# Attention and two gated layers on one core: one queue of decoding operations in place of parallel decoding, and the next segment's x split one cast at a time

## The chip, the core and the metric

The kernel runs on one core of a Trainium2 chip. The time is that of one execution on the device, in microseconds. The profile is of one execution, taken by the hardware profiler. The engines are TensorE (PE in the profile, its weight loads PEld), VectorE (DVE), ScalarE (ACT), GpSimd (POOL) and SyncE (SP), which issues nearly all DMAs. Each engine works through its own instructions in program order.

## The reference

Three layers in float32: masked attention over 4 batches, 8 heads, 576 positions and 64 dimensions; then two gated layers on 2304 tokens with 512 channels and 1536 hidden units, the first after an RMS norm. Cut to what matters:

```python
attn = softmax(where(mask, q @ k.T / 8, -1e9));  x = attn @ v          # (2304, 512)
xn = x / rms(x) * rms_g
y   = (silu(xn @ w_gate) * (xn @ w_val)) @ w_out                       # moe:  512 -> 1536 -> 512
out = (silu(y @ w2_gate) * (y @ w2_val)) @ w2_out                      # moe2: 512 -> 1536 -> 512
```

## The kernel before, in words

A float32 factor of a product is kept as two parts, a rounded high part and the rest (types F32R), and each product is three matmuls: high by high, high by low, low by high. Hidden units go in chunks of 128, twelve in each layer.

**Early part.** The attention and the first six chunks of the first gated layer run together, over six blocks of tokens (`segs`). The profile shows it up to about 399 us.

**Segments.** The rest is 15 segments (`work`) of 768 tokens: chunks 6 to 8 of the first layer for three blocks of tokens, chunks 9 to 11 for three, and for the second layer chunks 0 to 3, 4 to 7 and 8 to 11, for three blocks each. They are numbered 0 to 14 here; 0 to 5 have 3 chunks and 198 matmuls, 6 to 14 have 4 chunks and 240. In a segment a chunk's gate and value products (2 by 2 blocks of 384 tokens) are formed from seven block products, called steps 1 to 7 (`Chunk.step`), in the order 1, 2, 6, 5, 7, 4, 3. A step is six matmuls. Between steps ACT and DVE copy, add and take the SiLU of banks of PSUM: after step 1 ACT seeds a second bank (`seed`), after 6 and 7 it keeps a copy (`keep`), after 2 and 4 it applies the SiLU, and `join` makes the two parts of the hidden values (`hh` by ACT, `hl` by DVE). Down products follow a chunk or two later (`Half.down`); half of those of a segment are done in the next one (`left`).

**x of the next segment.** `stage_x` loads it into the one buffer `xst`, `sum_x` forms sums on POOL, and `split_q` makes for each of the seven steps two high parts (an ACT cast, `xh`, L984) and two low parts (a POOL subtraction, `xl`, L985). A tile of the split has one buffer, so it can be written once the last chunk of the running segment is past that step.

**Weights.** They are decoded from two 16 bit halves. A load takes one of three `raw` buffers, then come `low` and `high` (ACT, L198 and L190), `sign` and `join` (DVE, L202 and L207), then for each part of 512 or 256 columns a cast on ACT (`hi`, L214) and a subtraction on DVE (`lo`, L218). For the seven-step chunks `combined_step` loads gate and value weights together (two raws), and between decoding and the third cast POOL forms four differences (`sums`, L253). `weight_step` does the down weights. In the second layer `low` can go to a spare bank of PSUM (`lws`). There are 20 places for decoded weights of 4 KB and 5 of 2 KB; a chunk takes four and one, and gives them back when the last segment of its pass has used it.

**What sets the order.** `point()` is called twice in a step and once in each group of down products. There every weight step that is under way advances by one phase (all of them side by side, up to as many as the raw buffers allow), and by `pace["dec"]`, 0.25 per call, the next one is begun. Four empty phases lie between load and first operation. In this kernel the queue for the 18 later chunks holds combined weights and down weights by turns. A scheduler with priorities then orders each engine's instructions; `behind(engine)` keeps an instruction behind the last bank operation recorded for an engine. The next x is split by `split_next(z)` right after the last chunk's step z: four instructions at once, and their ACT casts are not held behind anything.

Of the kernel before, what the change touches and what calls it, by code (L numbers as in the profile page):

```python
# [25 lines left out]
def attn_ffn_ffn(ctx: ExitStack, tc: tile.TileContext, q, k, v, w1g, w1v, w1o, rms_g, w2g, w2v, w2o, out):  # L26
# [91 lines left out]
        if st:  # L118
            active.append(st)

    pace = {"att": 0.0, "dec": 0.0}
    have = {"att": 0.0, "dec": 0.0}

    def point():
        advance()
        for nm, src in (("dec", wq), ("att", steps)):
            if state["hold"] and nm == "dec":
                continue
            have[nm] = min(have[nm] + pace[nm], 2.0)
            while have[nm] >= 1.0 and src and src[0].ready():  # L130
                have[nm] -= 1.0
                start(src.pop(0))
# [87 lines left out]
    def weight_step(m, c, z):  # L220
        cell = {}

        def load():
            cell["at"] = take((m, c, z == 2), 4)
            cell.update(fetch(m, c, z))

        def first():
            cell["t"] = home(cell["at"], 512, f"w{m}_{c}_{z}")
            hi(cell["t"], cell["h"])

        def second():
            lo(cell["t"], cell["h"])
            wt[m, c, z] = cell["t"]
            wdone.add((m, c, z))

        return Step([load] + [wait] * 4 + scale(cell) + [first, second], lambda: room[4] and raws[0] >= 1, PRIO_W)

    def combined_step(m, c):

        g, v = {}, {}  # L240
        at = []

        def load():
            at.extend([take((m, c, False), 4) for _ in range(3)] + [take((m, c, False), 2)])
            g.update(fetch(m, c, 0))
            v.update(fetch(m, c, 1))

        def sums():
            t = g["raw"].rearrange("p k f -> p (k f)").bitcast(F32).rearrange("p (a n) -> p a n", a=4)
            b11, b21 = g["h"][:, 0:256], g["h"][:, 256:512]  # L250
            b12, b22 = v["h"][:, 0:256], v["h"][:, 256:512]
            for z, a, b in ((0, b12, b11), (2, b22, b12), (1, b22, t[:, 0]), (3, b21, t[:, 1])):
                nc.gpsimd.tensor_tensor(out=t[:, z], in0=a, in1=b, op=ALU.subtract)  # L253
            flat = t.rearrange("p a n -> p (a n)")
            g["parts"] = [(g["h"], 512, at[0]), (v["h"][:, 256:512], 256, at[3]), (flat[:, 0:512], 512, at[1]), (flat[:, 512:1024], 512, at[2])]
            g["t"] = []

        def first(i):
            def f():
                src, w, place = g["parts"][i]  # L260
                t = home(place, w, f"w{m}_{c}_{i}")
                g["t"].append(t)
                hi(t, src)
            return f

        def second(i):
            def f():
                lo(g["t"][i], g["parts"][i][0])
                if i == 3:
                    raws[0] += 1  # L270
                    tg, tb, t12, t34 = g["t"]
                    wt[m, c, 0] = {1: tg[:, :, 0:256], 2: tg[:, :, 256:512], 3: tb, 5: t12[:, :, 0:256], 6: t12[:, :, 256:512],
                                   7: t34[:, :, 0:256], 4: t34[:, :, 256:512]}
                    wdone.add((m, c, 0))
            return f

        return Step([load] + [wait] * 4 + scale(g, 0) + scale(v) + [sums, wait] +
                    [f(i) for i in range(4) for f in (first, second)],
                    lambda: len(room[4]) >= 3 and room[2] and raws[0] >= 2, PRIO_W)

# [2 lines left out]
        return tc.issue_after(last[eng]) if eng in last else nullcontext()  # L283

    def need_w(m, c, z):
        drain(wq, lambda: (m, c, z) in wdone)


    class Attention:
# [613 lines left out]
    for si, (m, t0, n, c0, c1) in enumerate(segs):  # L903
        nxt = segs[si + 1] if si + 1 < len(segs) else None
        loaded = False
        pace["att"] = 0.8 if si < 2 else 1.2
        pace["dec"] = 0.5 if si == NA - 1 else 0.25
        xs = xs_of.pop(si)
        state["tanh"] = True and att is not None
        for c in range(c0, c1):  # L910
            h = gate(m, c, n, xs)
            if si == last_seg[m, c]:
                used((m, c, False))
            if len(waiting) >= 2:
                run(waiting.pop(0))
            waiting.append((si, c, h))
            if att and not steps and not active_att():
                actx.close()
                att = None
                GV.append(("a0", "a1"))  # L920
                open_pool("x7", "x7", 0, bufs=1)
                open_pool("wpb", "wpb", 0, bufs=1)
                open_pool("ob", "ob", 512, bufs=4)
                room[4] += [(pools["wpb"][0], f"v{i}") for i in range(2)]
                room[2] += [(pools["wpb"][0], f"e{i}") for i in range(5)]
            if nxt and c >= c1 - 3 and si + 1 not in xs_of:
# [12 lines left out]
    while waiting:  # L939
        run(waiting.pop(0))  # L940
    pace["dec"] = 0.3
    close_pools(0, 1, "h")


# [26 lines left out]

    SRC = {1: "a11", 2: "a12", 3: "a12", 4: "a22", 5: "s1", 6: "a11", 7: "a21"}

    def split_q(cell, i, eng=nc.gpsimd):

        src = cell[SRC[i]]
        if i == 6:
            combine(eng, src, cell["s1"], src, ALU.subtract)
        if i == 3:
            combine(eng, src, src, cell["a11"], ALU.subtract)  # L980
        xh = x7.tile([128, 2, HN], F32R, tag=f"h{i}", name="xh")
        xl = x7.tile([128, 2, HN], F32R, tag=f"l{i}", name="xl")
# [148 lines left out]
    cell = stage_x(1, 0)  # L1131
    sum_x(cell, nc.vector)
    for i in (1, 2, 6, 5, 7, 4, 3):
        split_q(cell, i, nc.vector)
    left = []
    for n, (m, cs, t0) in enumerate(work):
        if t0 == 0:
# [9 lines left out]

        G = [J[:2], J[2:]]

        def split_next(i):  # L1150
            if nxt:
                split_q(cell, i)

        def step(c, z):
            c.step(z)
            if c is chunks[-1]:
                split_next(z)

        def lower(i, g):
            if i >= 0:  # L1160
                for j in G[g]:
                    halves[0].down(chunks[i].c, j, chunks[i].ha)
                point()

        def piece(hf, c, js, done):
            def f():
# [7 lines left out]
        def other_done(m=m, cs=cs, t0=t0):  # L1174
            if t0 + 2 * HN == NT:
                for c in cs:
                    used((m, c, True))

        def blank():
            if left:  # L1180
                left.pop(0)()

        for z in (1, 0, 0, 2, 6, 0, 5, 7, 0):
            step(chunks[0], z) if z else blank()
            if z == 2:
                spare[:] = ya[halves[0].n:]
        for i, c in enumerate(chunks[:-1]):
            c1 = chunks[i + 1]
            step(c1, 1)
            step(c, 4)  # L1190
            step(c, 3)
            if t0 + 2 * HN == NT:
                used((m, c.c, False))
            step(c1, 2)
            if i == 0 and nxt:
# [12 lines left out]
            lower(i, 0)  # L1208
# [12 lines left out]
        lower(k - 1, 0)  # L1221
        lower(k - 1, 1)
        blank()
        while nxt is None and left:
            blank()
    close_pools(*reversed(list(opened)))
# [30 lines left out]
```

## Time and profile before

| | us |
|---|---|
| median of 3 runs | 1063.78 (1061.88 to 1070.92) |
| the profiled execution | 1068.32, span 1065.7 |
| PE busy | 998.5 (94%) |
| PEld, DVE, ACT, POOL busy | 903.5, 584.4, 575.0, 443.0 |
| mean granted TensorE clock | 0.969 of full |

A busy share of PE holds matmuls whose ends are modelled and overlap, so a full window says only that PE was not seen to wait. Of the chain of work that ended last PE has 60% of the span, DMA 11%, ACT 9%, DVE 8%, POOL 7%.

### The profile page before, as it was taken

The page shows a single profiled execution, that of the slowest core. Times are in us where ns is not written, and L with a number is a line of the kernel's source. Part 1 is how long each engine was busy: PE and PEld are TensorE (multiplying, and loading weights), DVE is VectorE, ACT ScalarE, POOL GpSimd, SP SyncE. Part 2 cuts the span into 40 slices and gives each one's busy share as a digit, 9 for nine tenths or more (in the row PEclk, how much of TensorE's full clock was granted, in tenths as well). Part 3 has the DMA queues.
Part 4 walks back from the last instruction along what each step waited for, and adds up shares of the span by engine and source line. Part 5 has one row for each costly group of instructions (what it writes and reads, how often), then busy time and mean ns, then how long its engine had stood idle before and what let it go on. Part 6 is the DMA issues. An engine that isn't in the chain of part 4 may idle for free.

```text
span 1065.7 us, 16395 instructions
## 1 busy us (share of the span) xinstructions
PE 998.5 (94%) x5804; PEld 903.5 (85%) x5804; DVE 584.4 (55%) x1311; ACT 575.0 (54%) x1435; POOL 443.0 (42%) x463
## 2 busy tenths in 40 slices
PE   5758999999999998999899989999989999999998
PEld 4647998788789888898799978999888999889997
DVE  3777546354443767646685587333856337653433
ACT  4877646635623557446565356454846347562431
POOL 3212102103100132785796584643747264654600
PEclk9658999999999998999999999999999999999999
DMA  6575143241132346534644544303273433515021
GB/s 180 167 213 150 56 124 85 84 128 40 41 108 81 112 161 195 173 105 152 208 137 157 178 144 160 109 11 122 86 256 102 155 126 131 196 42 177 23 88 59
DMA packets 130090, 133.85 MB, mean 126 GB/s; under 512 B 41428, under 2 KB 113820, under 8 KB 130008
## 3 DMA queue, kind: packets, MB, share of 16 engines
q1 hardware_dynamic: 129816, 132.53, 38.9%
q8 instruction: 45, 0.74, 0.3%
q14 instruction: 37, 0.30, 0.1%
q0 software_dynamic: 192, 0.28, 0.1%
HBM read 99.75 MB, written 33.03 MB: 125 GB/s over the span
## 4 chain that ended last, share of the span: by engine, by line
PE 60%; DMA 11%; ACT 9%; DVE 8%; POOL 7%; issue 3%; SPq 2%; ACTq 0%; DVEq 0%; POOLq 0%
PE b_y L66 23%; PE b_a L66 14%; PE b_g L66 11%; PE b_v L66 10%; DMA raw<-in_moe_w_out_dram 6%; POOL xl L985 4%; DMA raw<-in_moe_w_gate_dram 2%; PE b_a L69 2%; ACT xh L984 2%; POOL raw L253 2%; DVE dh L207 2%; DMA raw<-in_moe_w_val_dram 2%; ACT w L214 2%; DMA xst<-x_d 1%; ACT raw L198 1%
## 5 line engine op out<-in xcount | busy, mean ns | idle before, releaser
L985 POOL TENSOR_TENSOR xl<-xst,xh 128x384 fp32r<-128x384 f32 x168 | 180.1, 1103 | 75.0 <-ACT xh L984 75.0
L66 PE MATMUL b_y<-xh,w 128*128 128x384 f32 x700 | 191.2, 338 | 10.7 <-ACT t L1008 5.5
L66 PE MATMUL b_g<-xh,w 128*128 128x384 f32 (+2 forms) x496 | 151.4, 353 | 5.0 <-DVE sg L753 2.7
L66 PEld LDWEIGHTS b_y<-xh,w 128*128 128x128 f32 x700 | 128.1, 188 | 17.7 <-ACT t L1008 9.5
L66 PE MATMUL b_v<-xh,w 128*128 128x384 f32 (+2 forms) x432 | 130.0, 351 | 4.4 <-ACT b_v L1014 2.6
L66 PE MATMUL b_a<-xh,w 128*128 128x384 f32 (+2 forms) x460 | 126.1, 336 | 3.3 <-ACT t L1008 2.8
L66 PE MATMUL b_y<-hh,w 128*128 128x256 f32 (+2 forms) x432 | 117.4, 343 | 0.5 <-ACT hh L1032 0.5
L66 PE MATMUL b_y<-xl,w 128*128 128x384 f32 x350 | 117.6, 336 | 0.0
L66 PEld LDWEIGHTS b_g<-xh,w 128*128 128x128 f32 x496 | 92.9, 195 | 14.3 <-ACT t L1008 4.9
L506 POOL TENSOR_TENSOR e<-e,rc 128x384 f32<-128x384 f32 (+3 forms) x40 | 38.5, 966 | 136.0 <-DVE rc L500 76.9
L984 ACT CAST xh<-xst 128x384 fp32r<-128x384 f32 x180 | 84.5, 518 | 14.1 <-POOL xst L965 10.5
L66 PEld LDWEIGHTS b_a<-xh,w 128*128 128x128 f32 x460 | 83.3, 188 | 8.1 <-ACT t L1008 4.5
L66 PEld LDWEIGHTS b_v<-xh,w 128*128 128x128 f32 x432 | 79.5, 192 | 12.0 <-ACT b_v L1014 2.9
L66 PE MATMUL b_g<-xl,w 128*128 128x384 f32 (+2 forms) x248 | 85.0, 343 | 0.0
L66 PEld LDWEIGHTS b_y<-hh,w 128*128 128x128 f32 x432 | 77.6, 190 | 6.7 <-ACT hh L1032 0.9
L965 POOL TENSOR_TENSOR s<-xst 128x384 f32<-128x384 f32 x28 | 29.8, 1086 | 122.7 <-DMA xst<-y_d 78.8
L253 POOL TENSOR_TENSOR raw<-dh 128x256 f32<-128x256 f32 x36 | 28.8, 818 | 122.6 <-DVE dh L207 119.5
L66 PE MATMUL b_a<-xl,w 128*128 128x384 f32 (+2 forms) x230 | 77.2, 336 | 0.0
L66 PE MATMUL b_y<-hl,w 128*128 128x256 f32 (+2 forms) x216 | 72.9, 338 | 1.5 <-DVE hl L1033 1.5
L66 PE MATMUL b_v<-xl,w 128*128 128x384 f32 (+2 forms) x216 | 73.5, 340 | 0.0
L489 ACT ACTIVATE e<-e,nb 128x96 f32<-128x96 f32 (+2 forms) x152 | 56.4, 372 | 21.7 <-DVE nb L480 21.5
L66 PEld LDWEIGHTS b_y<-xl,w 128*128 128x128 f32 x350 | 66.0, 189 | 1.8
(204 smaller groups left out, 2202.7 us busy)
## 6 DMA issues: line engine op xcount, KB each, us to landing
xst<-y_d SPq DMA_DIRECT2D x18, 768.0 KB
raw<-in_moe_w_gate_dram SPq DMA_DIRECT2D x24, 512.0 KB
raw<-in_moe_w_val_dram SPq DMA_DIRECT2D x24, 512.0 KB
raw<-in_moe_w_out_dram SPq DMA_DIRECT2D x24, 512.0 KB
part<-ob SPq DMA_DIRECT2D x48, 256.0 KB
ob<-part SPq DMA_DIRECT2D x36, 256.0 KB
ob<-part SPq DMA_DIRECT2D x32, 192.0 KB
part<-ob SPq DMA_DIRECT2D x24, 192.0 KB
```

The costliest lines, as they stand in the source:

```text
L66: traced(nc.tensor.matmul(out_, a, b_, start=start, stop=stop, **how))
L69: traced(nc.tensor.transpose(out_, a, one))
L198: nc.scalar.activation(out=cell["r"], in_=cell["lw"], func=AF.Copy, scale=LOW)
L207: nc.vector.scalar_tensor_tensor(out=h, in0=h, scalar=3, in1=cell["r"], op0=ALU.logical_shift_left, op1=ALU.bitwise_or)
L214: nc.scalar.copy(out=t[:, 0], in_=src)
L253: nc.gpsimd.tensor_tensor(out=t[:, z], in0=a, in1=b, op=ALU.subtract)
L489: r = nc.scalar.activation(out=e[:qn, i, :kn], in_=e[:qn, i, :kn], func=AF.Exp, bias=nb[:qn, i:i + 1], scale=-1.0, accum_out=sums[:qn, i:i ...
L506: eng.tensor_tensor(out=e[:qn, :nt, :kn], in0=e[:qn, :nt, :kn], in1=rc[:qn, :nt].unsqueeze(2).to_broadcast([qn, nt, kn]), op=ALU.mult)
L965: eng.tensor_tensor(out=out_[:, kk], in0=a[:, kk], in1=b[:, kk], op=op)
L984: nc.scalar.copy(out=xh[:, kk], in_=src[:, kk])
L985: eng.tensor_tensor(out=xl[:, kk], in0=src[:, kk], in1=xh[:, kk].bitcast(F32), op=ALU.subtract)
```

## The change

The matmuls and their order stay. Weight steps of the 18 later chunks go to a list `late`, in the order in which they are used, and are handled by two new functions. `prefetch` begins the first of the list (its load) as soon as buffers and places are there, without a pace. `operate` runs one operation of the oldest one begun; `weights()`, called at each `point()`, does as many as `pace["op"]` allows, and none until four calls after the load. So one weight step is decoded at a time, while the next ones are being loaded. The empty phases go. `stage_x` is called some six steps earlier, after step 5 of the first chunk. The casts of the split are held behind the last bank operation on ACT, and are handed out one at a time (list `due`), one after each product group. Core of the diff:

```diff
+    def prefetch(force=False):
+        if late and (late[0].ready() or force) and not wq:
+            st = late.pop(0)
+            phase(st, 0)
+            st.at = clock[0]
+            begun.append(st)
+
+    def operate():
+        phase(begun[0])
+        if not begun[0]:
+            begun.pop(0)
+
+    def weights():
+        clock[0] += 1
+        prefetch()
+        have["op"] = min(have["op"] + pace["op"], 2.0)
+        while have["op"] >= 1.0 and begun and clock[0] - begun[0].at >= 4:
+            have["op"] -= 1.0
+            operate()
 
     def point():
         advance()
+        weights()
...
-        return Step([load] + [wait] * 4 + scale(cell) + [first, second], lambda: room[4] and raws[0] >= 1, PRIO_W)
+        return Step([load] + scale(cell) + [first, second], lambda: room[4] and raws[0] >= 1, PRIO_W)
...
-        return Step([load] + [wait] * 4 + scale(g, 0) + scale(v) + [sums, wait] +
+        return Step([load] + scale(g, 0) + scale(v) + [sums] +
...
-    late = order[HC:]
-    for i, mc in enumerate(late):
-        wq.append(combined_step(*mc))
-        wq += [weight_step(*late[j], 2) for j in ((i - 1,) if i else ())]
-    wq.append(weight_step(*late[-1], 2))
+    late += [combined_step(1, c) if z == "c" else weight_step(1, c, 2) for z, c in
+             (("c", 6), ("c", 7), ("d", 6), ("c", 8), ("d", 7), ("d", 8), ("c", 9), ("d", 9), ("c", 10), ("d", 10), ("c", 11), ("d", 11))]
...
-        pace["dec"] = 0.5 if si == NA - 1 else 0.25
+        pace["dec"] = 0.25
+        pace["op"] = 1.5
...
-        for kk in range(2):
+        with nullcontext() if eng is nc.vector else behind("act"):
             nc.scalar.copy(out=xh[:, kk], in_=src[:, kk])
-            eng.tensor_tensor(out=xl[:, kk], in0=src[:, kk], in1=xh[:, kk].bitcast(F32), op=ALU.subtract)
-        xq[i] = xh, xl
+        eng.tensor_tensor(out=xl[:, kk], in0=src[:, kk], in1=xh[:, kk].bitcast(F32), op=ALU.subtract)
...
         def step(c, z):
             c.step(z)
-            if c is chunks[-1]:
-                split_next(z)
+            split_next()
+            if c is chunks[-1] and nxt:
+                due.extend(((z, 0), (z, 1)))
...
+        pace["op"] = 1.0 if m == 2 else 0.7 if n else 1.2
         for z in (1, 0, 0, 2, 6, 0, 5, 7, 0):
             step(chunks[0], z) if z else blank()
+            if z == 5 and nxt:
+                cell = stage_x(nxt[0], nxt[2])
...
             if i == 0 and nxt:
-                cell = stage_x(nxt[0], nxt[2])
                 sum_x(cell)
+            if i == k - 2:
+                pace["op"] = 0.35
```

What it does to the order of each engine, at three places. In the rows a name ends in a number of its own; `w1_8_0` is the decoded weight of layer 1, chunk 8, part 0 (part 2 is also the name of the down weights), `b_...` are banks.

ACT at the entry of segment 0, from the last `hh` of the early part to the first seed of the segment, before:

```order
L763 CAST hh_4343<-sg_4324 128x512
L198 ACTIVATE raw_4277<-raw_4277 128x512
L198 ACTIVATE raw_4312<-raw_4312 128x512
L190 ACTIVATE dh_4356<-raw_4277 128x512
L214 CAST w1_8_0_4405<-dh_4326 128x512
L76 COPY ob_4411<-b_y1_4153 128x512
L190 ACTIVATE dh_4358<-raw_4312 128x512
L76 COPY ob_4419<-b_y3_4155 128x512
L214 CAST w1_7_2_4390<-dh_4358 128x512
L1014 COPY b_v_4498<-b_g_4490 128x384
```

and now:

```order
L793 CAST hh_4359<-sg_4333 128x512
L239 CAST w1_8_2_4365<-raw_4262 128x512
L239 CAST w1_8_3_4380<-raw_4262 128x512
L223 ACTIVATE raw_4279<-raw_4279 128x512
L215 ACTIVATE dh_4396<-raw_4279 128x512
L223 ACTIVATE raw_4335<-raw_4335 128x512
L239 CAST w1_7_2_4416<-dh_4396 128x512
L76 COPY ob_4423<-b_y1_4164 128x512
L76 COPY ob_4431<-b_y3_4166 128x512
L1048 COPY b_v_4510<-b_g_4502 128x384
```

Chunk 8's parts 2 and 3, which came after the seed, now stand ahead of it, and no decoding operation stands between the two output copies and the seed.

ACT in segment 2, from the second chunk's copy t2 to the SiLU after the third chunk's step 2, before:

```order
L1008 COPY t2_5431<-b_a0_5369 128x384
L198 ACTIVATE raw_5405<-raw_5405 128x512
L198 ACTIVATE raw_5409<-raw_5409 128x512
L190 ACTIVATE dh_5445<-raw_5405 128x512
L190 ACTIVATE dh_5447<-raw_5409 128x512
L1008 COPY t3_5452<-b_a0_5369 128x384
L198 ACTIVATE raw_5407<-raw_5407 128x512
L1014 COPY b_v_5477<-b_g_5467 128x384
L984 CAST xh_5482<-xst_5416 128x384 x2
L1022 ACTIVATE b_a0_5369<-b_a0_5369 128x384
L214 CAST w1_10_2_5472<-dh_5447 128x512
L1022 ACTIVATE t1_5530<-b_v_5477 128x384
```

and now:

```order
L1042 COPY t2_5439<-b_a0_5383 128x384
L223 ACTIVATE raw_5419<-raw_5419 128x512
L215 ACTIVATE dh_5446<-raw_5419 128x512
L1042 COPY t3_5458<-b_a0_5383 128x384
L223 ACTIVATE raw_5421<-raw_5421 128x512
L1048 COPY b_v_5478<-b_g_5470 128x384
L215 ACTIVATE dh_5480<-raw_5421 128x512
L1056 ACTIVATE b_a0_5383<-b_a0_5383 128x384
L1066 CAST hh_5490<-b_a0_5383 128x384
L1013 CAST xh_5495<-xst_5370 128x384
L1056 ACTIVATE t1_5528<-b_v_5478 128x384
L239 CAST w1_11_0_5530<-dh_5446 128x512
```

Five decoding operations of three loads become four of two; the cast of a decoded weight moves from in front of the SiLU to behind it, and `hh` comes straight after its SiLU.

SP in segments 8 and 9, from the last stores of segment 8's outputs to a load of the down weights of chunk 6 of the second layer (`raw_8302` before, `raw_8380` now), before:

```order
L1129 DMA part2_1920_0_0_8367<-ob_8365 128x512
L1129 DMA part2_1920_1_0_8374<-ob_8372 128x512
L959 DMA xst_8485<-y_d768_6498 128x4x384
L959 DMA xst_8485<-y_d1152_6519 128x4x384
L1085 DMA ob_9172<-part2_768_0_0_7815 128x512
L181 DMA raw_8302<-in_moe2_w_out_dram 128x1024
```

and now:

```order
L1163 DMA part2_1920_0_0_8355<-ob_8353 128x512
L1163 DMA part2_1920_1_0_8362<-ob_8360 128x512
L206 DMA raw_8380<-in_moe2_w_out_dram 128x1024
L991 DMA xst_8412<-y_d768_6506 128x4x384
L991 DMA xst_8412<-y_d1152_6529 128x4x384
L206 DMA raw_8435<-in_moe2_w_out_dram 128x1024
```

The load of these down weights moves from behind the two loads of x to ahead of them. PE's order is the same in both kernels from its first row to its last, and ACT, DVE, POOL and SP have theirs unchanged through nearly all of the early part.

## Rows read from the trace of the kernel before

**Rows 1.** The page, busy time: us (share of the span) and instructions.

```profile
PE 998.5 (94%) x5804; PEld 903.5 (85%) x5804; DVE 584.4 (55%) x1311; ACT 575.0 (54%) x1435; POOL 443.0 (42%) x463
```

**Rows 2.** Stretches, one per segment: us, each engine's busy us (instructions), PEclk, DMA, GB/s.

```profile
399.30:444.10 44.80, 38.86 (x199) 36.90 (x198) 32.89 (x52) 30.36 (x64) 26.06 (x27) 0.92 0.53 170
444.10:478.40 34.30, 34.30 (x199) 34.30 (x199) 13.88 (x26) 15.55 (x35) 23.13 (x24) 1.00 0.42 140
478.40:518.10 39.70, 37.23 (x200) 35.45 (x199) 26.22 (x38) 21.90 (x48) 26.43 (x23) 0.96 0.45 143
518.10:559.00 40.90, 36.27 (x200) 34.10 (x199) 30.16 (x47) 24.84 (x54) 31.87 (x31) 1.00 0.57 187
...
593.30:634.10 40.80, 36.34 (x200) 34.09 (x199) 28.10 (x40) 22.59 (x49) 28.31 (x26) 1.00 0.41 135
...
682.00:727.90 45.90, 45.90 (x243) 42.83 (x242) 15.65 (x28) 19.88 (x44) 21.51 (x22) 1.00 0.21 69
...
774.80:827.00 52.20, 48.61 (x242) 43.94 (x241) 31.12 (x50) 28.11 (x62) 30.83 (x33) 0.97 0.52 175
...
sum 662.70, PE 636.61 PEld 594.22 DVE 366.86 ACT 347.54 POOL 369.18; mean PE 42.44 PEld 39.61 DVE 24.46 ACT 23.17 POOL 24.61
```

**Rows 3.** Waits of PE, 399 to 1062 us: us in total, times, longest.

```profile
PE b_y L66 <- ACT t L1008: 5.5, 9, 1.8
PE b_y L66 <- ACT t L1022: 4.8, 3, 2.3
...
PE b_v L66 <- ACT b_v L1014: 2.6, 1, 2.6
```

**Rows 4.** Waits of ACT, 399 to 1062 us.

```profile
ACT w L214 <- POOL raw L253: 33.7, 17, 5.3
...
ACT w L214 <- DVE dh L207: 14.4, 11, 4.2
```

**Rows 5.** Timeline, 398 to 404 us (start, us, engine, line, idle before and releaser).

```profile
400.65 0.66 ACT L190 ACTIVATE dh<-raw 128x512 f32<-128x512 f32 x1 [1.93 <-POOL raw L253]
401.21 0.57 ACT L76 COPY ob<-b_y 128x512 f32<-128x512 f32 x1
...
402.58 0.47 ACT L1014 COPY b_v<-b_g 128x384 f32<-128x384 f32 x1
...
403.11 0.69 PE L66 MATMUL b_v<-xh,w 128*128 128x384 f32 x1 [2.59 <-ACT b_v L1014]
```

**Rows 6.** Timeline, 489 to 501 us, in segment 2.

```profile
492.65 3.53 DVE L202 SCALAR_TENSOR_TENSOR raw<-raw 128x512 uint32<-128x512 uint32 x3
...
494.18 2.88 POOL L965 TENSOR_TENSOR xst<-xst 128x384 f32<-128x384 f32 x2
...
496.11 2.91 DVE L207 SCALAR_TENSOR_TENSOR dh<-dh,raw 128x512 uint32<-128x512 uint32 x2
...
499.06 0.62 ACT L214 CAST w<-dh 128x512 fp32r<-128x512 f32 x1 [4.18 <-DVE dh L207]
...
500.12 0.45 PE L66 MATMUL b_v<-xh,w 128*128 128x384 f32 x1 [1.76 <-ACT t L1022]
```

**Rows 7.** Timeline, 521 to 527 us, at the start of segment 3.

```profile
522.04 0.62 ACT L214 CAST w<-raw 128x512 fp32r<-128x512 f32 x1 [2.37 <-POOL raw L253]
...
523.65 0.44 PE L66 MATMUL b_y<-xh,w 128*128 128x384 f32 x1 [2.25 <-ACT t L1022]
```

**Rows 8.** Timeline, 786 to 792 us, in segment 9.

```profile
789.15 0.67 ACT L198 ACTIVATE raw<-raw 128x512 uint32<-128x512 uint32 x1 [2.63 <-DMA raw<-in_moe_w_out_dram]
...
790.23 0.45 PE L66 MATMUL b_y<-xh,w 128*128 128x384 f32 x1 [1.80 <-ACT t L1008]
```

**Rows 9.** DVE by line and shape, 395 to 1060 us: count, busy us, mean ns.

```profile
L207 DVE SCALAR_TENSOR_TENSOR dh<-dh,raw 128x512 uint32<-128x512 uint32 x29 | 29.0, 1007 | 6.0 <-ACT dh L190 5.4
...
L207 DVE SCALAR_TENSOR_TENSOR dh<-dh,lws 128x512 uint32<-128x512 uint32 x19 | 12.9, 679 | 1.3 <-ACT dh L190 1.2
```

**Rows 10.** POOL by line and shape, 395 to 1060 us.

```profile
L985 POOL TENSOR_TENSOR xl<-xst,xh 128x384 fp32r<-128x384 f32 x168 | 180.1, 1103 | 75.0 <-ACT xh L984 75.0
```

More of the change, by code (lines that the diff above doesn't have):

```diff
@@ L119, in start @@
             active.append(st)
-    pace = {"att": 0.0, "dec": 0.0}
-    have = {"att": 0.0, "dec": 0.0}
+    pace = {"att": 0.0, "dec": 0.0, "op": 0.0}
+    have = {"att": 0.0, "dec": 0.0, "op": 0.0}
+    late = []
+    begun = []
+    clock = [0]
+    def prefetch(force=False):
[15 more added lines that the diff above has]
+            operate()
     def point():
         advance()
+        weights()
         for nm, src in (("dec", wq), ("att", steps)):
@@ L285, in need_w @@
     def need_w(m, c, z):
-        drain(wq, lambda: (m, c, z) in wdone)
+        drain(wq, lambda: (m, c, z) in wdone or not wq and not any(st.prio == PRIO_W for st in active))
+        while (m, c, z) not in wdone:
+            if begun:
+                operate()
+            else:
+                prefetch(True)
     class Attention:
@@ L861, in attn_ffn_ffn @@
     wq += [weight_step(1, c, z) for c in range(HC) for z in range(3)]
-    late = order[HC:]
-    for i, mc in enumerate(late):
-        wq.append(combined_step(*mc))
-        wq += [weight_step(*late[j], 2) for j in ((i - 1,) if i else ())]
-    wq.append(weight_step(*late[-1], 2))
+    late += [combined_step(1, c) if z == "c" else weight_step(1, c, 2) for z, c in
+             (("c", 6), ("c", 7), ("d", 6), ("c", 8), ("d", 7), ("d", 8), ("c", 9), ("d", 9), ("c", 10), ("d", 10), ("c", 11), ("d", 11))]
+    late += [combined_step(2, c) if z == "c" else weight_step(2, c, 2) for z, c in
[3 rows of a table added]
     att.consts()
@@ L940, in attn_ffn_ffn @@
         run(waiting.pop(0))
-    pace["dec"] = 0.3
+    pace["op"] = 1.0
     close_pools(0, 1, "h")
@@ L972, in attn_ffn_ffn, with split_q @@
     SRC = {1: "a11", 2: "a12", 3: "a12", 4: "a22", 5: "s1", 6: "a11", 7: "a21"}
-    def split_q(cell, i, eng=nc.gpsimd):
+    def split_q(cell, i, kk, eng=nc.gpsimd):
         src = cell[SRC[i]]
[L977 to L982, printed above, removed]
-        for kk in range(2):
-            nc.scalar.copy(out=xh[:, kk], in_=src[:, kk])
-            eng.tensor_tensor(out=xl[:, kk], in0=src[:, kk], in1=xh[:, kk].bitcast(F32), op=ALU.subtract)
-        xq[i] = xh, xl
+        if kk == 0:
+            cell[i] = x7.tile([128, 2, HN], F32R, tag=f"h{i}", name="xh"), x7.tile([128, 2, HN], F32R, tag=f"l{i}", name="xl")
+        xh, xl = cell[i]
+        with nullcontext() if eng is nc.vector else behind("act"):
+            nc.scalar.copy(out=xh[:, kk], in_=src[:, kk])
+        eng.tensor_tensor(out=xl[:, kk], in0=src[:, kk], in1=xh[:, kk].bitcast(F32), op=ALU.subtract)
+        if kk == 1:
+            xq[i] = xh, xl
+            if i == 1:
+                combine(eng, src, cell["s1"], src, ALU.subtract)
+            if i == 2:
+                combine(eng, src, src, cell["a11"], ALU.subtract)
     def tmp(tag, bufs):
@@ L1133, in attn_ffn_ffn @@
     for i in (1, 2, 6, 5, 7, 4, 3):
-        split_q(cell, i, nc.vector)
+        split_q(cell, i, 0, nc.vector)
+        split_q(cell, i, 1, nc.vector)
     left = []
@@ L1148, in attn_ffn_ffn, with split_next @@
         G = [J[:2], J[2:]]
-        def split_next(i):
-            if nxt:
-                split_q(cell, i)
+        def split_next():
+            if due:
+                split_q(cell, *due.pop(0))
         def step(c, z):
             c.step(z)
-            if c is chunks[-1]:
-                split_next(z)
+            split_next()
+            if c is chunks[-1] and nxt:
+                due.extend(((z, 0), (z, 1)))
         def lower(i, g):
@@ L1163, in lower @@
                 point()
+                split_next()
         def piece(hf, c, js, done):
@@ L1177, in other_done @@
                     used((m, c, True))
+        due = []
         def blank():
@@ L1181, in blank @@
                 left.pop(0)()
+            split_next()
+        pace["op"] = 1.0 if m == 2 else 0.7 if n else 1.2
         for z in (1, 0, 0, 2, 6, 0, 5, 7, 0):
             step(chunks[0], z) if z else blank()
+            if z == 5 and nxt:
+                cell = stage_x(nxt[0], nxt[2])
             if z == 2:
@@ L1223, in attn_ffn_ffn @@
         blank()
+        while due:
+            split_next()
         while nxt is None and left:
```

3 rows, old and new, of the table att are left out of this document.

## The prediction, made before the changed kernel had run

> **What bounds the kernel now.** I read the page first. PE is busy for 998.5 of 1065.7 us [rows 1], so this is a kernel of one engine, and only what makes PE wait, or slows it, can be won. Next the waits by engine and stretch: the early part has waits too, but the order of the program there hardly changes, so I leave it at its time and look at the segments, from 399.3 us to 1062.0 us.
>
> The view by stretches, one per segment, gives the measure for that part. Segments 0 to 5 have the same 198 matmuls, 6 to 14 the same 240. Where no weights are decoded, segment 1 takes 34.3 us and segment 7 45.9 us, and PE fills both [rows 2]. I take these as the time of an undisturbed segment. All 15 take 662.7 us [rows 2]; 6 x 34.3 + 9 x 45.9 = 618.9. So **43.8 us is what the segments lose**, and it is lost where weights are decoded: 10.5 us in segment 0, 5.4 in segment 2, 6.6 in 3, 6.5 in 5, 6.3 in 9 [rows 2], together 35.3, and by difference 8.5 in the other ten, most of it in 6, 8, 11 and 12.
>
> What is waited for: PE's waits in the segments are mostly for ACT, for the copies (L1008), the SiLU (L1022) and one seed (L1014), not for data of its own [rows 3]. And ACT itself waits, at the cast of a decoded weight, 33.7 us for POOL's differences and 14.4 us for DVE [rows 4]. ACT runs in order, so a cast that waits holds every copy and SiLU behind it. That is the whole pattern: decoding operations stand in ACT's queue ahead of what PE needs, and their inputs are late. Part of the loss is clock: after such a wait the granted clock of the segment falls, to a mean of 0.92 in segment 0, 0.96 in segment 2 and 0.97 in segment 9 [rows 2], that is 44.8 x 0.08 = 3.6 us, 39.7 x 0.04 = 1.6 and 52.2 x 0.03 = 1.6 us.
>
> **The change part by part.** No matmul is added, removed or moved. Neither are there more or fewer decoding operations, casts or subtractions: 48 words' halves are joined in the segments [rows 9], and the program has as many joins as before. What changes is the place of ACT's, DVE's, POOL's and SP's instructions against each other, so I price each disturbed segment by the wait that its rows show and ask whether the new order still has it.
>
> *Entry of segment 0.* ACT stands 1.93 us at a decoding activation, since POOL has not finished the differences that read the buffer to be written; the output copy and the seed come after it, and PE waits 2.59 us [rows 5]. In the new order no decoding operation stands between the copies and the seed, and the differences are asked for earlier. The second output copy (0.57 us) cannot start before PE's last down product, and the seed takes 0.47 us [rows 5], so about 0.7 us of wait stays. Back: 2.59 - 0.7 = 1.9 us, and the 3.6 us of clock. The remaining 4.3 us of this segment are small waits; ACT's decoding operations in the segment go from 25 to 19 by the order, so I take a quarter of them, 1.0. Sum 6.5.
>
> *Segment 2.* DVE needs 3.53 us for three and 2.91 us for two operations while POOL sums x; the cast waits 4.18 us for them, and the SiLU behind it lets PE wait 1.76 us [rows 6]. Now the loads' operations come one at a time and the cast stands behind the SiLU. Back: 1.76 + 1.6 of clock, and of the other 2.0 us a quarter, 0.5. Sum 3.9.
>
> *Segment 3.* A cast waits 2.37 us for POOL's differences and PE 2.25 us behind it [rows 7]. Here the new order helps less: between the differences and the cast that reads them there were five calls of `point`, there are now four operations, at 0.7 per call some six calls. I take half of 6.6: 3.3.
>
> *Segment 5* repeats the order of segment 2 without the loss of clock; 60% of 6.5: 3.9.
>
> *Segment 9.* A load of down weights, queued behind two loads of x, holds ACT for 2.63 us and PE for 1.80 [rows 8]. Now it is issued ahead of them. Back: 1.80 + 1.6 of clock, and 0.4 of the remaining 2.9. Sum 3.8.
>
> *The other segments* have 8.5 us; I take 30%, 2.6.
>
> *Given back.* Decoding goes on into segments 1 and 4, which were free of it (5 and 9 operations on ACT where 0 and 1 stood), and into the last chunk of segment 6 (5 where none stood), beside the 14 casts. Bounds for a segment newly touched: 0 (segment 1 shows that the casts alone cost nothing [rows 2]) and 6 us (what a segment full of decoding loses). The five or nine operations are nearer the first: 1.0 for segments 1 and 4 together, 1.0 for the last chunks. Minus 2.0.
>
> *x loaded earlier, casts held back.* The load is taken off the path of the sums, which waited for it; POOL has no part in the end of a segment, being busy 23 of 34 us in segment 1 [rows 2]. I cost both at nothing. What hides them is that the split of the last steps is used some ten matmul groups into the next segment; without that cover a late subtraction costs 1.1 us each [rows 10].
>
> Sum: 6.5 + 3.9 + 3.3 + 3.9 + 3.8 + 2.6 - 2.0 = **22.0 us**. The profiled execution took 1068.3 us, so it would take 1046.3. It lies 4.5 us above the median of the runs, 1063.8; from that the prediction is **1042 us**. Ends of the terms: nothing at all comes back (1064) and everything does (1020).
>
> **The rivals.** *All of it goes.* If ACT is never held, the segments fall to 34.3 and 45.9 us: 1063.8 - 43.8 = 1020. Against it: 33.7 us of ACT's waits are for POOL's differences [rows 4], and these stay, with one phase less ahead of them. I count all results under 1028 here: 7%.
>
> *The waits only move.* Only what the order visibly clears comes back: 1.9 + 3.6 at the entry, 1.76 + 1.6 in segment 2, together 8.9, less 3 for the newly touched segments: 1058. That the change does not do what it says belongs here: three raw buffers still limit the loads, so that the steady rate could be a queue that waits for DMA. For it: loads are issued by the same queue and as large as before. Against it: the one example in the rows moves ahead. From 1053 to 1074: 15%.
>
> *Slower: DVE and POOL in each other's way.* Decoding operations whose inputs are all in SBUF take 1007 ns, those with one in PSUM 679 ns for the same shape [rows 9], and while POOL is at work three took 3.53 and two 2.91 us, some 1.45 each, the last of them [rows 6]. A steady rate spreads decoding over the time in which POOL splits x; each of the operations then costs 1.45 - 0.68 = 0.77 us more, and two of them, sign and join, ahead of the multiplication that `hh` needs hold ACT for 1.5 us, now that nothing stands between SiLU and `hh`. Where that makes PE wait about as long as in segment 2, it costs what it cost there, 1.76 + 1.6 of clock: in the ten segments with decoding 34 us, against 22 won: 12 slower, 1076. It decides if such a wait falls in most segments, and not in some: from seven on the gain is gone. Against it: each such wait is spread too, and an undisturbed chunk leaves DVE idle for 60% of the time (13.88 of 34.3 us busy [rows 2]). 7%. The Trainium skill, page "SBUF — State Buffer", section "Who interferes with whom", states such a rule: an operation of VectorE with both inputs in SBUF and one of GpSimd that reads SBUF share a port pair by an exclusive lock, and the loser waits for the whole instruction. The trace agrees: 0.68 us of its own and most of one POOL instruction make 1.45 us. By that rule alone, applied to every such operation, the time would be this rival's.
>
> **How the numbers follow.** The forecast, with 12 to 36 us back, 1028 to 1052, has 71%; all of it goes 7%; the waits only move 15%; slower 7%. The range of 1027 to 1058 leaves out about 6% below and some 14% above. A change of over 1% (10.6 us) can be told from none: faster is the first two, 78%; no change takes the third and a little of the last, 15%; slower 7%.
>
> **What would show it.** In segment 0 PE's wait for the seed at the entry should be under 1 us and the granted clock 1.00. Segments 2 and 9 should have a clock of 0.99 or more, and segments 2, 3, 5 and 9 take under 37, 38, 37 and 49 us. ACT's waits at the cast of a weight, 33.7 for POOL and 14.4 for DVE, should fall by more than half for DVE and less for POOL. Segments 1 and 4 should stay within 1 us of 34.3. PE's busy count and matmuls must be the same. The prediction is wrong if the decoding segments keep more than half of their 43.8 us, or if segments 1, 4, 7, 10 and 13 grow; for the slower rival, if DVE's sign and join reach 1.45 us on average and `hh` waits behind them.

## The result, and the profile after

The changed kernel takes **1048.99 us** (median of 4 runs, 1045.32 to 1051.62) where the one before took 1065.16 in the same rounds: ratio 0.985, 95% interval 0.980 to 0.989. That is 1.1 to 2.0% faster, inside the forecast range (1027 to 1058) and less of a gain than the point forecast (1042). The profiled execution took 1045.32 us with a span of 1043.5.

First the page, busy time and instructions, to be laid beside [rows 1]:

```profile
PE 986.0 (94%) x5804; PEld 899.1 (86%) x5804; DVE 589.0 (56%) x1311; ACT 575.2 (55%) x1435; POOL 448.0 (43%) x463
```

Every engine has as many instructions as before, so nothing but their places has changed. PE is busy for 12.5 us less with the same products, 7.3 of it in the segments (636.6 to 629.3 in the sums of the next view).

Next the segments by stretch, the answer to [rows 2] (us; busy us and instructions of PE, PEld, DVE, ACT and POOL; PEclk; DMA; GB/s). Shown are segments 0 to 6, 9 and 12:

```profile
395.20:433.80 38.60, 35.66 (x200) 34.12 (x199) 30.53 (x49) 28.71 (x62) 20.08 (x21) 1.00 0.55 177
433.80:471.80 38.00, 36.12 (x199) 35.80 (x198) 19.09 (x31) 16.76 (x38) 27.44 (x27) 0.96 0.48 153
471.80:506.20 34.40, 34.40 (x201) 34.40 (x200) 21.16 (x34) 20.13 (x44) 22.07 (x22) 1.00 0.45 142
506.20:546.70 40.50, 36.90 (x200) 35.66 (x199) 29.25 (x43) 24.17 (x52) 31.63 (x30) 0.96 0.57 183
546.70:581.30 34.60, 34.60 (x200) 34.25 (x199) 21.08 (x36) 19.41 (x43) 29.22 (x30) 1.00 0.60 193
581.30:615.60 34.30, 34.30 (x199) 34.30 (x198) 20.83 (x34) 20.06 (x44) 22.52 (x22) 1.00 0.45 142
615.60:667.30 51.70, 48.04 (x242) 43.94 (x241) 36.09 (x55) 32.32 (x69) 36.30 (x37) 0.97 0.45 147
...
759.50:808.10 48.60, 46.78 (x242) 42.48 (x241) 35.49 (x56) 30.79 (x66) 33.00 (x33) 1.00 0.57 193
...
900.20:947.50 47.30, 46.15 (x242) 42.74 (x241) 28.27 (x46) 25.05 (x55) 29.06 (x29) 1.00 0.38 131
...
sum 644.60, PE 629.33 PEld 594.33 DVE 368.24 ACT 346.21 POOL 370.92; mean PE 41.96 PEld 39.62 DVE 24.55 ACT 23.08 POOL 24.73
```

The segments lost 43.8 us to decoding; now it is 644.6 - 618.9 = 25.7. Segments 2 and 5 are whole, 0 and 9 are shorter, but segments 1 (34.3 before) and 6 (47.9 before) have grown by 3.7 and 3.8 us, and 3 has hardly moved. The clock's loss has moved with them, from segments 0, 2 and 9 to 1, 3 and 6.

What ACT's casts of weights wait for in the segments (us in total, times, longest), the answer to [rows 4]:

```profile
ACT w L239 <- POOL raw L278: 20.4, 9, 3.8
ACT w L239 <- DVE dh L232: 8.0, 11, 1.4
```

Fewer and shorter than the 33.7 and 14.4 us of before, but the two largest of PE's waits still stand behind them. In segment 3 (timeline: start, us, engine, line, idle before and releaser):

```profile
523.19 1.98 POOL L997 TENSOR_TENSOR s<-xst 128x384 f32<-128x384 f32 x2 [8.87 <-DMA ob<-part]
...
525.12 1.44 POOL L278 TENSOR_TENSOR raw<-dh 128x256 f32<-128x256 f32 x2
...
526.53 2.42 POOL L997 TENSOR_TENSOR xst<-xst 128x384 f32<-128x384 f32 x2
...
528.90 0.72 POOL L278 TENSOR_TENSOR raw<-dh,raw 128x256 f32<-128x256 f32 x1
...
529.66 0.62 ACT L239 CAST w<-raw 128x512 fp32r<-128x512 f32 x1 [2.83 <-POOL raw L278]
...
530.75 0.47 ACT L1042 COPY t<-b_y 128x384 f32<-128x384 f32 x1
...
531.27 0.69 PE L66 MATMUL b_y<-xh,w 128*128 128x384 f32 x1 [3.19 <-ACT t L1042]
```

Read upward from PE: it waits for a copy, the copy stands behind a cast, the cast behind POOL's third difference. POOL does that difference in 0.72 us, but two operations on x (2.42 us) stand ahead of it, and ahead of those the sums of x, before which POOL was idle for 8.87 us until transfers had landed. The same picture in segment 1:

```profile
435.52 1.50 DVE L232 SCALAR_TENSOR_TENSOR dh<-dh,raw 128x512 uint32<-128x512 uint32 x1
...
440.24 0.72 POOL L278 TENSOR_TENSOR raw<-dh,raw 128x256 f32<-128x256 f32 x1
440.99 0.62 ACT L239 CAST w<-raw 128x512 fp32r<-128x512 f32 x1 [3.32 <-POOL raw L278]
441.52 0.47 ACT L1042 COPY t<-b_y 128x384 f32<-128x384 f32 x1
...
442.04 0.44 PE L66 MATMUL b_y<-xh,w 128*128 128x384 f32 x1 [1.89 <-ACT t L1042]
```

There the difference stands behind six subtractions of the split of x, which hold POOL from 432.60 to 440.28 us. Segment 6 has its long wait in the first third, again behind subtractions of the split (five, until 624.19 us):

```profile
626.50 0.62 ACT L239 CAST w<-raw 128x512 fp32r<-128x512 f32 x1 [3.77 <-POOL raw L278]
...
629.80 0.45 PE L66 MATMUL b_a<-xh,w 128*128 128x384 f32 x1 [2.53 <-ACT t L1056]
```

### The profile page after: what moved, and what is told of

It reads as the page before. It is cut to its first block, busy times and chain, and to the rows that moved or that the text cites. A ratio compares the mean times of both kernels' runs of the same rounds, so it can differ in the third digit from the quotient of the medians.

```text
span 1043.5 us, 16408 instructions
## 1 busy us (share of the span) xinstructions
PE 986.0 (94%) x5804; PEld 899.1 (86%) x5804; DVE 589.0 (56%) x1311; ACT 575.2 (55%) x1435; POOL 448.0 (43%) x463
## 4 chain that ended last, share of the span: by engine, by line
PE 63%; POOL 9%; ACT 8%; DMA 8%; DVE 5%; issue 3%; SPq 2%; DVEq 0%; POOLq 0%; ACTq 0%
PE b_y L66 25%; PE b_a L66 15%; PE b_g L66 11%; PE b_v L66 10%; POOL xl L1014 5%; POOL raw L278 2%; DMA raw<-in_moe_w_gate_dram 2%; DMA xst<-x_d 2%; PE b_a L69 2%; DMA raw<-in_moe_w_out_dram 2%; POOL xst L997 2%; ACT e L519 2%; ACT w L239 1%; ACT dh L215 1%; ACT raw L223 1%
## 5 line engine op out<-in xcount | busy, mean ns | idle before, releaser
L1014 POOL TENSOR_TENSOR xl<-xst,xh 128x384 fp32r<-128x384 f32 x168 | 183.6, 1123 | 78.7 <-PE b_y L66 39.7
L66 PE MATMUL b_g<-xh,w 128*128 128x384 f32 (+2 forms) x496 | 147.9, 346 | 3.9 <-DVE sg L783 2.7
L66 PEld LDWEIGHTS b_g<-xh,w 128*128 128x128 f32 x496 | 90.8, 191 | 11.1 <-DVE sg L783 2.9
L997 POOL TENSOR_TENSOR s<-xst 128x384 f32<-128x384 f32 x28 | 29.7, 1083 | 100.3 <-DMA xst<-y_d 63.6
```

The costliest lines, as they stand in the source:

```text
L66: traced(nc.tensor.matmul(out_, a, b_, start=start, stop=stop, **how))
L997: eng.tensor_tensor(out=out_[:, kk], in0=a[:, kk], in1=b[:, kk], op=op)
```

## The experiments

All were timed in five rounds against the kernel before. For single segments I give the time from a segment's first product to the next one's, read from the one trace of each kernel and good to 0.1 us.

**One part alone.** Decoding as changed, with the split and the x load as before:

> The new decoding (one queue, list in the order of need, loads ahead) with the old split of x: four instructions at once, casts not held behind bank operations, x loaded at the old place. If the gain comes from the decoding, as the prediction's terms have it: 1049 to 1053, within 4 us of the changed kernel. If the held casts carry it: 1058 to 1065. If the two need each other: in between, near 1056.

It took 1050.43 us, ratio 0.985 (0.982 to 0.988), the segments 646.7. The split and the load as changed, with the decoding as before:

> The new split and the earlier load of x with the old decoding (all steps side by side, four empty phases, old list, old pace). If the decoding carries the gain: 1060 to 1066, no change from the kernel before. If the held casts carry it: 1049 to 1054. ACT's wait at the cast of a weight for DVE (14.4 us before) should stay above 10 us under the first, and fall under the second.

It took 1079.99 us, ratio 1.013 (1.010 to 1.017): slower. Its segments sum to 674.2 us, and PE waits for what the changed kernel never lets it wait for there:

```profile
PE b_g L66 <- POOL xl L1006: 11.9, 3, 5.0
PE b_y L66 <- POOL xl L1006: 9.6, 2, 5.0
```

So the decoding carries 16.0 of the 18.1 us, and the held-back split is free only with it. The two parts do not add: the split costs 11.5 us of segments beside the old decoding (674.2 - 662.7) and gives 2.1 beside the new. What in the decoding does it (one load at a time, the order of the list, the paces) no run here separates.

The 2.1 us are a difference of larger shifts. With the decoding alone segments 1 and 6 take 35.0 and 48.8 us, against 38.0 and 51.7 in the changed kernel, while 0, 2, 3, 4 and 5 are 1.2 to 2.4 us longer. In that run segment 1 begins at 441.8 us, and POOL's six subtractions of x end 1.3 us later; in the changed kernel it begins at 433.8, and they end 6.5 us later, with a difference of weights behind them. In segment 6 they end 2.0 and 8.6 us after its start.

```profile
441.80:476.80 35.00, 34.63 (x200) 34.31 (x199) 16.65 (x31) 17.56 (x39) 24.18 (x25) 1.00 0.52 167
...
627.40:676.20 48.80, 47.22 (x242) 42.25 (x242) 32.61 (x56) 33.30 (x70) 31.09 (x33) 1.00 0.45 149
...
436.76 6.32 POOL L1017 TENSOR_TENSOR xl<-xst,xh 128x384 fp32r<-128x384 f32 x6
```

**The x load at its old place.** `stage_x` goes back to where `sum_x` is called:

```
-            if z == 5 and nxt:
-                cell = stage_x(nxt[0], nxt[2])
...
             if i == 0 and nxt:
+                cell = stage_x(nxt[0], nxt[2])
                 sum_x(cell)
```

> The changed kernel with the load of x back at its old place, right before the sums. The prediction costed the earlier load at nothing: 1048 to 1051, same as the changed kernel. Rival: the later load lets POOL begin its sums later, so that differences of weights queue behind them: 1053 to 1060.

1050.03 us, ratio 0.986 (0.983 to 0.989), segments 644.1: no difference in the sum, though segment 0 is 1.3 us longer than in the changed kernel, with a clock of 0.96 for 1.00, and segment 1 is 1.5 shorter, with 1.00 for 0.96 after the same wait of PE, 1.9 us. POOL waits for x all the same, 106.4 us in 13 sums against 97.6 in the changed kernel and 119.3 before (the waits for transfers of the sums at L997, before L965). The queue that issues the load waits, eight times in the changed kernel and 11.9 us in all, until POOL has read the one buffer of x for its last subtractions; an earlier call bought 9 us of POOL's idle time and nothing in the segments' sum.

**The differences on DVE**, `nc.gpsimd` to `nc.vector` for all four in one step:

> The changed kernel with the four differences of each combined weight on DVE, behind its last bank operation, in place of POOL. Theory: what is left of the loss is the cast of differences, which waits on ACT for POOL's queue; then segments 1, 3, 6, 9 and 12 lose their long waits (3.7, 6.2, 5.8, 2.7 and 1.4 us over the undisturbed time) and it takes 1034 to 1040. Rival, DVE and POOL in each other's way: DVE gets 64 more operations with both inputs in SBUF, at 0.4 to 1.2 us, while POOL is at work, and the time stays at 1046 to 1055 or grows.

1052.63 us, ratio 0.988 (0.985 to 0.991). No cast waits for POOL any more, and the second layer's nine segments take 418.0 us where they took 424.2. But segments 0, 2 and 5 are 44.5, 40.6 and 40.6 us. In segment 2:

```profile
495.55 4.05 POOL L1015 TENSOR_TENSOR xl<-xst,xh 128x384 fp32r<-128x384 f32 x3
...
497.50 2.38 DVE L279 TENSOR_TENSOR raw<-dh 128x256 f32<-128x256 f32 x2
...
499.81 2.34 DVE L279 TENSOR_TENSOR raw<-dh,raw 128x256 f32<-128x256 f32 x2
...
502.07 0.54 DVE L1053 TENSOR_TENSOR t<-t,b_v 128x384 f32<-128x384 f32 x1
...
502.67 0.69 PE L66 MATMUL b_v<-xh,w 128*128 128x384 f32 x1 [3.54 <-DVE t L1053]
```

Four differences hold DVE for 4.7 us, and PE's sum stands behind them: the wait has changed engines, and the rival's time is right. **In the second layer alone** on DVE, on POOL in the first:

> The changed kernel with the differences of the second layer's weights on DVE, those of the first on POOL as they were. In the run with all of them on DVE the second layer's nine segments took 418.0 us, in the changed kernel 424.4; the first layer's six took 245.0 against 220.4. Theory A (in the second layer POOL is late since it is splitting x and DVE has room; in the first it is the other way about): the first layer's segments that decode first-layer weights (0, 1 and 2) stay at 38.6, 38.1 and 34.3 us, the second layer's take 418 us, and the time falls by 3 to 6 us unless segments 3 to 5, which decode second-layer weights, take it back (40.6, 34.4 and 40.6 us in the run with all on DVE, against 40.5, 34.6 and 34.3). Rival B (they do take it back): segment 5 is 40 us and the time is within 2 us of the changed kernel's.

1045.93 us, ratio 0.984 (0.980 to 0.987). Rival B has it in segment 5: 39.5 us; the second layer's nine take 419.0. The segments sum to 645.6, no less than the changed kernel's.

**Single differences on DVE**, each a step of its own between the casts:

```
-scale(v) + [sums] + [f(i) for i in range(4) for f in (first, second)]
+scale(v) + [one(0), first(0), second(0), one(1), first(1), second(1), one(2), first(2), second(2), one(3), ...]
```

> The changed kernel with the four differences of each combined load on DVE instead of POOL, each a step of its own between the casts, where the run before had the four in one step. Theory A (with the four in one step, DVE is blocked for about 4.7 us and PE waits for a sum in PSUM, 7.3 us in three; single ones of 1.17 us fit between DVE's other work): segments 0, 2 and 5 fall from 44.5, 40.6 and 40.6 us to under 39, segments 9 and 12 stay at 46 to 47, and the time is 1040 to 1046. Rival B (DVE is the bound in the first layer's segments, and takes the same work however it is spread): these segments stay over 40 us each, and the time is 1048 to 1055.

1046.79 us, ratio 0.983 (0.978 to 0.987). Theory A holds for segments 2 and 5 (35.7 and 35.6), hardly for 0 (39.4) and not for 9 (50.3). The time lies between the two forecasts, and the segments sum to 637.2, the least of all runs. Segment 3 is cured with the differences out of POOL's queue and spread over DVE's; with all four in one step on DVE it had stayed at 40.6, since there the cast waits 3.05 us for DVE. Segment 9 now has DVE's wait:

```profile
506.70:542.70 36.00, 34.92 (x200) 34.21 (x199) 28.11 (x44) 23.00 (x49) 23.87 (x22) 1.00 0.59 194
...
754.30:804.60 50.30, 47.82 (x241) 43.89 (x241) 41.35 (x65) 31.90 (x68) 27.43 (x24) 0.97 0.53 176
```

**Later casts**, differences on POOL as they were, and four empty steps (`[wait] * 4`) ahead of the casts that read them:

> The changed kernel with four empty steps between a combined load's second and third difference part, so that the casts of these parts stand later in ACT's queue. Theory A (the loss that is left comes from the cast of the third difference part, which stands in ACT's queue before POOL has its differences): ACT's waits at the cast of a weight for POOL's differences, 20.9 us in the changed kernel, fall below 8 us; segments 1, 3, 6, 9 and 12 lose their waits of 2.2, 3.2, 2.5, 1.1 and 1.2 us and the clock after them, and the time falls by 6 to 12 us, to about 1040. Rival B (the loss is the decoding's own load on DVE and POOL, and a cast that stands later is only replaced by a later wait, of PE for the weight or of ACT for the next decoding): ACT's waits for POOL fall, and the segments' sum stays within 3 us of the changed kernel's 644.7.

1044.97 us, ratio 0.982 (0.979 to 0.985), segments 639.8, that is 4.8 less than the changed kernel's, more than rival B's 3; the time is 4.0 us less, where theory A gave 6 to 12. The casts' waits for POOL fell to 6.2 us as theory A says, and segments 1, 6, 9 and 12 fell to 35.6, 45.3, 47.2 and 46.6 us. Segment 7 grows to 49.2, since PE waits 3.1 us for one of POOL's subtractions of x, and segment 3 stays at 40.5. There rival B is right: behind the same four differences another of ACT's casts, that of x, waits for POOL:

```profile
525.11 1.43 POOL L278 TENSOR_TENSOR raw<-dh 128x256 f32<-128x256 f32 x2
526.50 1.54 POOL L278 TENSOR_TENSOR raw<-dh,raw 128x256 f32<-128x256 f32 x2
528.00 0.99 POOL L1015 TENSOR_TENSOR xl<-xst,xh 128x384 fp32r<-128x384 f32 x1
529.07 0.99 POOL L998 TENSOR_TENSOR xst<-s,xst 128x384 f32<-128x384 f32 x1
...
530.09 0.51 ACT L1014 CAST xh<-xst 128x384 fp32r<-128x384 f32 x1 [5.24 <-POOL xst L998]
530.51 0.47 ACT L1043 COPY t<-b_y 128x384 f32<-128x384 f32 x1
...
531.04 0.44 PE L66 MATMUL b_y<-xh,w 128*128 128x384 f32 x1 [3.71 <-ACT t L1043]
```

**No decoding at the entry of segment 0** (`pace["op"] = 0.0` while the last early work runs):

> The changed kernel with no decoding step at the entry of segment 0, while the last work of the early part is run. Theory A (the seed at the entry is late since a decoding cast ahead of the output copies waits 1.36 us for DVE's join): the gap of 2.72 us between matmuls at the entry falls to about 1 us and segment 0 takes 36.5 to 37.5 us, with the time 1 to 2 us under the changed kernel's. Rival B (the gap is the copies and the seed themselves): the gap stays over 2 us, and the decoding that was put off makes segments 0 and 1 longer by up to 2 us.

1051.02 us, ratio 0.987 (0.984 to 0.990). Half of each: PE's wait at the entry fell from 2.38 to 0.55 us (2.72 to 0.89 from start to start of the matmuls), so the late seed was the cast's doing. But segment 0 takes 40.0 us and 3 takes 42.2, against 38.6 and 40.5, and only segment 1 is shorter, 36.2 against 38.0. What was put off is missing later.

```profile
401.55 0.45 PE L66 MATMUL b_v<-xh,w 128*128 128x384 f32 x1 [0.55 <-ACT b_v L1050]
```

**Put together.** Late casts for the first layer, single differences on DVE two or three steps ahead of their casts for the second; then the latter for both layers; then two differences on each engine:

> The first layer's weights as in the run with late casts, the second layer's with single differences on DVE, each put two or three steps ahead of the cast that reads it. If segments add up as measured apart (0 to 2 from the run with late casts: 37.5, 35.6, 34.5; the rest from the run with single differences on DVE: 36.0, 35.8, 35.6, 46.8, 46.5, 46.8, 50.3 and 230), the segments sum to 635 and the time is 1037 to 1044. Rival (DVE's order shifts with every step that is moved, and the sums do not carry over): over 1045.

> Single differences on DVE for both layers, each two or three steps ahead of its cast. Theory (what is left is ACT's wait for the difference, 7.8 us at casts in the run where difference and cast stood side by side): ACT's waits for DVE's differences fall under 3 us, PE's waits for DVE's sum in PSUM stay near 7 us, and the time is 1040 to 1046. Rival (DVE is the bound where POOL splits x, and a longer lead only lets more of DVE's steps bunch): PE's waits for DVE over 10 us and the time over 1047.

> As the run before it, with two of each four differences on DVE and two on POOL, in single steps. Theory (both engines have queues that hold a difference up; half each halves both waits): ACT's waits for POOL and for DVE under 10 us together, and the time 1038 to 1045. Rival (each of the two stands in line for the other, since one difference reads another's result across the engines): waits on both, over 1047.

They took 1040.23, 1043.01 and 1042.77 us, ratios 0.979 (0.974 to 0.983), 0.978 (0.975 to 0.982) and 0.980 (0.976 to 0.984). The segments sum to 638.1, 639.9 and 639.6, so the first is short of the 635 that its parts gave apart: segment 6 is 48.7 for 46.8, 4 is 37.3 for 35.8. In the second, casts wait 4.0 us for DVE's differences, not the expected under 3, and the time is as expected; in the third they wait 5.5 for both engines together, and both expectations hold. None of the three sums is below the 637.2 of single differences on DVE, so putting parts together has gained nothing that the sums show. What PE still waits for in the first:

```profile
PE b_y L66 <- DVE t L1065: 3.5, 2, 2.5
PE b_y L66 <- ACT t L1055: 2.6, 3, 1.6
PE b_a L66 <- DVE t L1065: 2.1, 3, 1.2
```

**The changed kernel once more**, as a base in five rounds:

> The changed kernel itself, unedited, as the base for the runs above, on the rounds that they had. If the start of the segments is what scatters (394.6 to 401.9 us over ten executions, with an order that is the same in all of them) and the segments repeat, segments 1, 3, 6, 9 and 12 have their waits again at the same places, the sum of the segments is 642 to 648 us, and the median 1047 to 1051. If the waits are a matter of chance in one execution, these segments differ by more than 2 us from 38.1, 40.5, 51.7, 48.6 and 47.3.

1047.69 us, ratio 0.982 (0.979 to 0.986), and its segments repeat within 0.3 us each:

```profile
sum 644.50, PE 629.55 PEld 594.17 DVE 367.13 ACT 346.49 POOL 370.66; mean PE 41.97 PEld 39.61 DVE 24.48 ACT 23.10 POOL 24.71
```

In this one pair of traces the segments' sum repeats within 0.1 us, where the whole time scatters by 8. By that sum the three put together are 4.6 to 6.4 us better than the changed kernel, each from one trace (a fall of the clock that comes in one run and not in another, as in segment 1 above, moves such a sum by 1.5); by the whole times their intervals still overlap its own.

## Why the prediction came out as it did

The direction, and that the gain lies in the decoding segments, were right. 22.0 us were to come back in the segments, and 18.1 did. The point is 7 us off for three reasons: 3.9 us in the segments, 1.4 since the base was 1065.2 in these rounds, and about 1.7 elsewhere, which is less than the start of the segments scatters.

- *Segments 2, 5 and 9*: 3.9, 3.9 and 3.8 predicted; 5.3, 6.5 and 3.6 measured. The mechanism was right. In 2 and 5 everything came back, so "a quarter" and "60%" were too little; with the decoding alone they take 36.3 and 35.5 us, so 1.9 and 1.2 of that are the split's, which was costed at nothing.
- *Entry of segment 0*: 6.5 predicted, 6.2 measured, but made up otherwise, so the total is near by luck. The seed's wait was to fall to 0.7 us and is 2.38. A decoding cast stands ahead of the output copies here too, now for DVE's join:

```profile
396.75 0.62 ACT L239 CAST w<-dh 128x512 fp32r<-128x512 f32 x1 [1.36 <-DVE dh L232]
397.27 1.06 ACT L76 COPY ob<-b_y 128x512 f32<-128x512 f32 x2
...
398.23 0.49 ACT L1048 COPY b_v<-b_g 128x384 f32<-128x384 f32 x1
...
398.77 0.44 PE L66 MATMUL b_v<-xh,w 128*128 128x384 f32 x1 [2.38 <-ACT b_v L1048]
```

  The clock's 3.6 us did come back (1.00 in the stretch), 0.2 of the seed's wait in place of 1.9, and 2.4 of small waits in place of 1.0.
- *Segment 3*: **the first step that failed.** "I take half of 6.6: 3.3" came to 0.4. I counted the calls between difference and cast. What decides is what stands ahead of the difference in POOL's queue: sums that wait for x, then operations on x. Taking the differences out of that queue gave 4.5 us (36.0) where they were also spread singly over DVE, and none in one step (40.6); moving only the cast gave none.
- *Given back*: **the second, and the largest.** "Minus 2.0" was 7.8: 3.7 in segment 1, 0.3 in 4, 3.8 in 6. I priced newly touched segments by the number of ACT's operations, nearer 0 than 6. Segment 1 has few, 38 instructions on ACT against 35, but one cast behind a full POOL queue costs PE 1.89 us and the clock 38.0 x 0.04 = 1.5. In segment 6 the loss is in the first third and not in the last chunk, for which I had priced it. With the decoding alone these three segments lose 4.3 us (0.7, 2.7 and 0.9); the held-back split adds 3.0 and 2.9 in 1 and 6, where POOL's subtractions of x now reach into the first third, and takes 2.4 off 4. So the loss in 1 and 6 belongs mostly to the term that was costed at nothing.
- *The other segments*: 2.6 predicted, 3.9 measured, most of it in 12 (49.9 to 47.3).
- *x loaded earlier, casts held back*: nothing predicted; nothing measured for the load, and 2.1 us gained for both together, as the balance of shifts of 1.2 to 3.0 us in single segments. My reason for the load was wrong, though: POOL's sums still wait for x. And the cover of the split that I named holds only beside the new decoding: with the split alone PE waits for its subtractions five times, up to 5.0 us at a time, where I had priced 1.1 for each.
- *The rival of DVE and POOL in each other's way* has its price but not its reach. In segment 1 a join takes 1.50 us beside POOL's six subtractions, as the turns of [rows 6] did. The mean over all joins with both inputs in SBUF rose only from 1007 to 1042 ns:

```profile
L232 DVE SCALAR_TENSOR_TENSOR dh<-dh,raw 128x512 uint32<-128x512 uint32 x25 | 26.1, 1042 | 2.1 <-ACT dh L215 1.4
L232 DVE SCALAR_TENSOR_TENSOR dh<-dh,lws 128x512 uint32<-128x512 uint32 x22 | 15.1, 684 | 0.9
```

  The run with the four differences on DVE is that rival come true, in three segments: 0.96 to 1.19 us for each, where one that started between two of POOL's operations took 0.41 in the run with single differences. That agrees with the rule in the Trainium skill, page "SBUF — State Buffer", section "Who interferes with whom", which gives the shared pair to one engine for a whole instruction.
- *"All of it goes"* stayed out of reach: the run with the smallest sum still loses 637.2 - 618.9 = 18.3 us.
- *The signs I had named* are mixed. Segments 2, 5 and 9 keep to their bounds and the clock is 1.00 in 0, 2 and 9. But the seed's wait is not under 1 us, segment 3 is over 38, and the casts' waits for DVE fell by 44%, not by half. Two signs of being wrong came: the segments keep 25.7 of 43.8 us, more than half, and segment 1 grew. The sum was right in where the gain lies, and wrong in how much the moved work costs elsewhere.

What is shown: that POOL's and DVE's differences hold ACT's casts and through them PE, since moving the casts and moving the differences each took most of the waits where the theory put them (segment 3 with late casts and segment 9 with single differences are the exceptions above). What stays open is which part of the new decoding brings its 16.0 us, and why the clock falls after one such wait and not after another (below).

## What to carry to other kernels

Where one engine runs in order and serves the bound engine, price a moved instruction by the queue of whoever makes its input, not by the number of its own neighbours: the wait costs what stands ahead of the producer. Work spread evenly over segments that were free of it takes their slack too, so look there first for what is given back. Run the parts of a change apart and compare them stretch by stretch: a part whose sum is near nothing can hide a loss in one stretch and a gain in another. And when the whole time scatters more than the effect, sum a stretch that repeats.

## What the runs showed that I had not expected

The start of the segments, after an early part whose order the edits hardly touch, lay between 394.5 and 401.9 us over the profiled executions; it was 395.2 and 394.5 in two of the changed kernel, 399.3 before. So the early part's 4 us are no sure gain. Part of the scatter goes with the granted clock: from 75 to 100 us it is 0.59 in the runs with the two latest starts (401.9 and 400.2), 0.80 before, and 0.93 and 0.90 in the changed kernel; but the earliest but one (394.6) has 0.82, so it does not explain all.

The granted clock fell after PE's wait of 1.89 us in segment 1 (0.96 in the stretch) and after the 3.19 in segment 3, and not after the 2.38 at the entry of segment 0 (1.00). With late casts a wait of 3.08 us in segment 7 left it at 1.00 as well, and one of 3.71 in segment 3 took it to 0.96. With the load of x at its old place PE waits 1.9 us in segment 1 too, at the same copy, and the clock stays at 1.00. The length of the wait alone does not tell.
